# GEGLU gate and value in seven half-size products from block 4 on, with shared staging, in a fused cosformer attention and GEGLU kernel on one core

## The chip, the cores and the metric

One core of a Trainium2 chip. The metric is the device time of one execution in microseconds (us). The kernel before took 314.08 us, the median of three runs (313.26, 314.08, 315.52). The profiled execution has a span of 311.0 us, and all durations below are from it.

TensorE (PE) multiplies matrices into PSUM, which has eight banks of 128 x 512 f32. VectorE (DVE), ScalarE (ACT) and GpSimd (POOL) work on tiles, and SyncE (SP) issues most transfers. Each engine works its own instructions in order, and semaphores make it wait for others.

## What is computed

```python
# q, k, v: (8, 8, 576, 64); phi(x) = [relu(x) cos(theta), relu(x) sin(theta)], theta = pi/2 * s/576
q_p, k_p = phi(q), phi(k)                       # 128 features a head
kv = einsum('bhsf,bhsd->bhfd', k_p, v)
z = sum(k_p, axis=2)
num = einsum('bhsf,bhfd->bhsd', q_p, kv)
den = einsum('bhsf,bhf->bhs', q_p, z) + 1e-6
x = (num / den) -> (4608, 512)                  # 8 batches of 576 rows, 8 heads of 64
out = (gelu(x @ w_gate) * (x @ w_val)) @ w_out  # 512 -> 1536 -> 512
```

Inputs and output are f32; the matmuls take bf16 and sum in f32.

## The kernel before, in words

The 4608 rows of x are cut into nine blocks of 512 (n = 0 to 8). A block's gate and value are made in twelve units of 128 columns of d_ff (jt = 0 to 11, here also called slots, because the other work is placed between units). The order of all work is written out by hand (`tc.manual_schedule`): each engine's instructions run in the order in which the program issues them.

**Standard unit** (`gv_unit`, L392): four matmuls of 128 x 512 for the gate into one bank, four for the value into the next, ACT's gelu (L409), and DVE's product of the two into hT (L410). Units take turns on banks 0, 1 and 2, 3.

**Output product** (`product`, L503). The output of block n - 1 is made during block n, in two halves p of the rows, each in seven half-size products in place of eight (Winograd's form of Strassen's method). A product is six matmuls of 128 x 256 (L510). The slots of one half make products 2 and 1, 5, 6, 7, 4 and 3 in turn. Sums S1 to S4 of parts of hT are made on DVE (`h_sum`, L494), sums of the weights T1 to T4 once. ACT copies products 1, 6 and 7 to SBUF (u, L528), and DVE adds them to others (L524). Rows are stored by SP (L421).

**Attention** of batch b = n + 1 is done in the slots of block n. q and k are scaled by cosine on DVE (L163) and by sine on ACT (L161), 128 x 256 at a time, from f32 staging places (two buffers for each of q, k, v) that SP loads (`loads`, L81) two batches ahead. q is transposed by DMA (`turn_q`, L194); `kv_unit` (L242) makes kv in 72 small matmuls; `nm_unit` makes one of five tiles of num and den (8 matmuls, L283, always in banks 6 and 7 from block 2 on), and DVE makes den, its reciprocal and x (L294 to L296); x is transposed by DMA (`turn_x`, L350). In the blocks from 4 on kv is in slot 1, the nm's in slots 2 to 6, q's transposes in slot 8, and the scalings of batch n + 2 in slots 7 to 11; in block 3 batch 5's q is scaled in slots 5 to 9 and its k in slots 10, 11 and block 4's slot 0, after the load of both in slot 11 of block 2.

**Fast unit** (`fast_unit`, L599). The last 28 units, from slot 8 of block 6 on (`FAST`, L557), make gate and value as one 2 x 2 product: [w_gate; w_val], cut in two along d_model, times the block's rows cut in two. Seven products of two 128 x 256 matmuls each (L611) take the place of eight. This needs sums of the weights (`w_sum`, L575) and of x (`x_sum`, L591), and partial results pass through ACT copies and DVE adds. Unit t's first products are woven with the last ones of unit t - 1. The sums of the weights are made in blocks 5 and 6 and lie in the freed staging places of q, k and v.

Of the kernel before, what the change touches and what calls it, by code (L numbers as in the profile page):

```python
# [16 lines left out]
def kernel(  # L17
# [33 lines left out]
    inp = ctx.enter_context(tc.tile_pool(name="inp", bufs=2))  # L51
# [6 lines left out]
    outp = ctx.enter_context(tc.tile_pool(name="outp", bufs=4))  # L58
    psum = ctx.enter_context(tc.tile_pool(name="psum", bufs=1, space=bass.MemoryType.PSUM))
# [17 lines left out]

    def load(eng, name, b, m0, m1, j0=0, j1=R):
        if (name, b) not in staged:
            staged[name, b] = inp.tile([128, NP, R * D], FP32, name=name + "f")  # L80
        eng.dma_start(  # L81
            out=staged[name, b][:, m0:m1, j0 * D:j1 * D],
            in_=rows(srcs[name], b)[:, m0:m1, j0 * D:j1 * D],
        )
# [3 lines left out]
    wo_sb = weights.tile([128, JT, C], BF16)  # L88
    wg_r = moe_w_gate.rearrange("(ct p) j -> p ct j", p=128)
# [23 lines left out]
    dummy = consts.tile([128, BLK], BF16)  # L113
# [32 lines left out]
    phi = {}  # L146

    def phi_tile(name, b):
        if (name, b) not in phi:
            phi[name, b] = attn.tile([128, NP, R, F], BF16, name=name + "p")  # L150
        return phi[name, b]

    def prep(name, b, part, js, m0=0, m1=NP, eng=None):
# [3 lines left out]
        for j in js:  # L157
            o = dst[:, m0:m1, j, part * D:(part + 1) * D]
            i = src[:, m0:m1, j * D:(j + 1) * D]
            if eng is nc.scalar:  # L160
                nc.scalar.activation(o, i, AF.Relu, scale=tab[:, j:j + 1])  # L161
            else:
                (eng or nc.vector).tensor_scalar(  # L163
                    o, i, 0.0, tab[:, j:j + 1], op0=ALU.max, op1=ALU.mult
                )

# [225 lines left out]
    def gv_unit(n, jt, c0=0, w=BLK):  # L392
        xt = xT[n]
        js = slice(jt * 128, (jt + 1) * 128)
        b0 = 2 * (turn[0] % 2)
        turn[0] += 1
        if n not in hT:
            hT[n] = ffn.tile([128, JT, BLK], BF16, name="hT")
        for g, wt in ((0, wg_sb), (1, wv_sb)):
            for ct in range(CT):  # L400
                nc.tensor.matmul(  # L401
                    bank(b0 + g)[:, 0:w],
# [5 lines left out]
        gel = ffn.tile([128, BLK], FP32, name="gel")  # L408
        nc.scalar.activation(gel[:, 0:w], bank(b0)[:, 0:w], AF.Gelu)  # L409
        nc.vector.tensor_mul(  # L410
            hT[n][:, jt, c0:c0 + w], gel[:, 0:w], bank(b0 + 1)[:, 0:w]
# [58 lines left out]
    hs, rest = {}, {}  # L470

    def place(n, p, name, cols, dtype):

        if n < NB - 1:
            return sums.tile([128, cols], dtype, name=name)
        was = "kp" if name[0] == "u" else ("kf", "vf")[p]
        if was not in rest:
            pool, n_el = (attn, 8 * CH) if was == "kp" else (inp, 4 * JH * 128)
            rest[was] = [pool.tile([128, n_el], dtype, name=was), 0]
        t, at = rest[was]  # L480
        rest[was][1] += cols
        return t[:, at:at + cols]
# [74 lines left out]
    FAST = (NB - 3) * JT + 8  # L557
    UNITS = NB * JT - FAST
    CP = CT // 2
    wa, xb, temps = {}, {}, {}  # L560

    def w_sum(name, j0, j1, eng=nc.vector):
        if not wa:
            wa["A11"], wa["A12"] = wg_sb[:, 0:CP], wg_sb[:, CP:CT]
            wa["A21"], wa["A22"] = wv_sb[:, 0:CP], wv_sb[:, CP:CT]
        if name not in wa:
            was = {"S1": "qf", "S2": "qf", "S3": "kf", "S4": "vf"}[name]
            wa[name] = inp.tile([128, CP, J], BF16, name=was)
# [6 lines left out]
        eng.tensor_tensor(  # L575
            wa[name][:, :, j0:j1], wa[x][:, :, j0:j1], wa[y][:, :, j0:j1], op=op
        )

    def x_sum(n, i):
        if n not in xb:  # L580
            xt = xT[n]
            xb[n] = {
                "B11": xt[:, 0:CP, 0:256], "B12": xt[:, 0:CP, 256:512],
                "B21": xt[:, CP:CT, 0:256], "B22": xt[:, CP:CT, 256:512],
            }
        if "x" not in temps:
            temps["x"] = attn.tile([128, 2, 4, CP, 256], BF16, name="qp")
        b = xb[n]
        x, y = (("B12", "B11"), ("B22", "T1"), ("B22", "B12"), ("B21", "T2"))[i]
        b[f"T{i + 1}"] = temps["x"][:, n % 2, i]  # L590
        nc.vector.tensor_tensor(b[f"T{i + 1}"], b[x], b[y], op=ALU.subtract)  # L591
# [5 lines left out]
    gels = {}  # L597

    def fast_unit(t, between):  # L599


        def at(i, t):
            if i == 2:
                return ps[:, 0, 256 * (t % 2):256 * (t % 2) + 256]
            return bank((3, 1)[t % 2] if i in (3, 5) else (2, 6, 7)[t % 3])[:, 0:256]

        def mm(i, t):
            n, jt = divmod(FAST + t, JT)
            a, b = GV[i]
            for ct in range(CP):  # L610
                nc.tensor.matmul(  # L611
                    at(i, t),
                    lhsT=wa[a][:, ct, jt * 128:(jt + 1) * 128],
                    rhs=xb[n][b][:, ct],
                    start=(ct == 0 and i in (1, 5)),
                    stop=(ct == CP - 1),
                    skip_group_check=i not in (1, 5),
                )

        def tmp(i, t):  # L620
            if "t" not in temps:
                temps["t"] = attn.tile([128, 6, 256], FP32, name="qT")
            return temps["t"][:, 2 * i + t % 2]

        def h(t, half):
            n, jt = divmod(FAST + t, JT)
            if n not in hT:
                hT[n] = ffn.tile([128, JT, BLK], BF16, name="hT")
            return hT[n][:, jt, 256 * half:256 * half + 256]

        def gelu(t, half, src):
            if t not in gels:
                gels[t] = ffn.tile([128, BLK], FP32, name="gel")
            nc.scalar.activation(gels[t][:, 256 * half:256 * half + 256], src, AF.Gelu)

        new, old = t < UNITS, t > 0
        M5, U6, G2 = range(3)
        if new:
            mm(1, t)
            nc.scalar.copy(at(2, t), at(1, t))  # L640
            mm(5, t)
            nc.scalar.copy(tmp(M5, t), at(5, t))
        if old:
            mm(7, t - 1)
            gelu(t - 1, 1, tmp(G2, t - 1))
            nc.vector.tensor_tensor(at(3, t - 1), tmp(M5, t - 1), at(7, t - 1), op=ALU.add)
            nc.vector.tensor_tensor(
                h(t - 1, 1), gels[t - 1][:, 256:512], at(3, t - 1), op=ALU.mult
            )
        between()  # L650
        if new:
            mm(6, t)
            nc.scalar.copy(tmp(U6, t), at(6, t))
            mm(2, t)
            gelu(t, 0, at(2, t))
            mm(3, t)
            nc.vector.tensor_tensor(tmp(G2, t), tmp(U6, t), at(3, t), op=ALU.add)
        if old:
            mm(4, t - 1)
            nc.vector.tensor_tensor(  # L660
                h(t - 1, 0), gels[t - 1][:, 0:256], at(4, t - 1), op=ALU.mult
            )
# [33 lines left out]
    for name in ("q", "k"):  # L696
        for m in (0, 2):
            load(nc.gpsimd, name, 2, m, m + 2)
    for m in (0, 2):
        load(nc.gpsimd, "v", 2, m, m + 2)  # L700
# [54 lines left out]
    for jt in range(2, 4):  # L755
        gv_unit(0, jt)
        prep("q", 0, jt - 2, (R - 1,), eng=nc.scalar)
    q1 = {9: (0, 1, 2), 10: (3, 4, 5), 11: (6, 7, 8)}
    for jt in range(4, JT):
        gv_unit(0, jt)  # L760
        if jt == 5:
# [5 lines left out]
        if jt in q1:  # L767
            prep("q", 1, 0, q1[jt])
            prep("q", 1, 1, q1[jt], eng=nc.scalar)

# [267 lines left out]
```

## Time and profile before

| | before |
|---|---|
| runs | 313.26, 314.08, 315.52 us |
| span of the profiled execution | 311.0 us |
| instructions | 7704 |
| units: standard, fast | 80, 28 |
| mean of a standard unit's gelu on ACT, 128 x 512 | 593 ns |
| mean of a scaling on ACT, 128 x 256 | 498 ns |
| landing time of a k load, of 12 on SP | 7.2 us median on the page |
| landing time of an output store | 2.5 us |

The profile has no figure of the profiled execution's own time apart from its span; the runs lie 2.3 to 4.5 us above it. A line such as `L401 PE MATMUL ps<-xT,wv_sb 128*128 128x512 bf16 (+1 forms) x338 | 80.6, 359 | 0.2` gives the source line, the engine, output and inputs by tile name, the shape, how many there were, busy time in us, mean ns of one, and the engine's idle time before them. The 40 slices of the span show when engines work:

```profile
PE   8889999999999999999999999999999999999993
DVE  5954686699897997799688878899899787978782
ACT  7854685966564763365525932593328787787830
POOL 6775420000000000000000000000007991297310
```

Each digit is the busy share of 7.8 us, in tenths. POOL has nothing to do between the first loads and the sums of the weights.

### The profile page before, as it was taken

The numbers are of one execution on the slowest core, as the hardware profiler recorded it, in microseconds if no ns is written. First come the engines' busy times: TensorE is split into PE (matmuls) and PEld (weight loads), VectorE is DVE, ScalarE is ACT, GpSimd is POOL, SyncE is SP. The second block draws the span as 40 slices with busy tenths as digits, with TensorE's granted clock in tenths as the row PEclk, the third lists the DMA queues.
The fourth block names the chain that finished last, engine by engine and source line by source line (L and its number), as shares of the span: only waits on it lengthen the run. The fifth ranks groups of instructions, "written<-read, shape, count | busy, mean of one in ns | idle before, by whom it ended". The sixth has DMA issues, their size and how long they took to land.

```text
span 311.0 us, 7704 instructions
## 1 busy us (share of the span) xinstructions
PE 301.0 (97%) x2867; PEld 208.2 (67%) x2895; DVE 246.8 (79%) x622; ACT 186.6 (60%) x468; POOL 67.9 (22%) x70
## 2 busy tenths in 40 slices
PE   8889999999999999999999999999999999999993
PEld 3574456645876676666666566656668888888882
DVE  5954686699897997799688878899899787978782
ACT  7854685966564763365525932593328787787830
POOL 6775420000000000000000000000007991297310
PEclk9999999999999999999999999999999999999999
DMA  7999999971798956993898589538442111202034
GB/s 277 247 186 246 313 315 412 273 145 37 217 225 260 315 132 153 368 232 94 259 291 177 116 277 303 112 83 124 93 106 52 40 32 41 50 21 69 3 80 123
DMA packets 69077, 53.65 MB, mean 172 GB/s; under 512 B 45392, under 2 KB 54352, under 8 KB 69040
## 3 DMA queue, kind: packets, MB, share of 16 engines
q1 hardware_dynamic: 59264, 41.17, 52.0%
q0 software_dynamic: 9696, 11.93, 16.5%
q8 instruction: 22, 0.36, 0.5%
q14 instruction: 15, 0.12, 0.1%
q10 hardware_dynamic: 80, 0.07, 0.1%
HBM read 37.75 MB, written 9.44 MB: 152 GB/s over the span
## 4 chain that ended last, share of the span: by engine, by line
PE 87%; DMA 4%; issue 4%; POOL 2%; DVE 0%; SPq 0%; ACT 0%; POOLq 0%; ACTq 0%; DVEq 0%
PE ps L401 43%; PE ps L510 20%; PE ps L611 13%; PE ps L431 3%; PE ps L283 3%; PE ps L242 3%; DMA vf<-in_v_dram 2%; DMA wv_sb<-in_moe_w_val_dram 2%; POOL kf L494 1%; PE ps L373 1%; PE ps L205 1%; PE ps L358 0%; SPq L81 0%; POOL gate L679 0%; POOL wg_sb L95 0%
## 5 line engine op out<-in xcount | busy, mean ns | idle before, releaser
L401 PE MATMUL ps<-xT,wv_sb 128*128 128x512 bf16 (+1 forms) x338 | 80.6, 359 | 0.2
L401 PE MATMUL ps<-xT,wg_sb 128*128 128x512 bf16 (+1 forms) x326 | 79.5, 358 | 1.1 <-issue 0.3
L409 ACT ACTIVATE gel<-ps 128x512 f32<-128x512 f32 (+1 forms) x86 | 47.7, 556 | 46.5 <-PE ps L401 43.3
L410 DVE TENSOR_TENSOR hT<-gel,ps 128x512 bf16<-128x512 f32 (+1 forms) x86 | 54.0, 633 | 24.0 <-PE ps L401 19.2
L401 PEld LDWEIGHTS <-wv_sb 128*128 128x128 bf16 x344 | 33.6, 98 | 33.9
L401 PEld LDWEIGHTS <-wg_sb 128*128 128x128 bf16 x344 | 30.7, 98 | 20.9 <-issue 0.2
L974 POOL CAST gate<-qp 128x1 f32<-128x1 bf16 x1 | 0.2, 175 | 190.7 <-DVE qp L591 190.7
L510 PEld LDWEIGHTS <-S 128*128 128x128 bf16 x336 | 32.9, 98 | 10.9 <-DVE S L494 0.6
L528 ACT COPY u<-ps 128x256 f32<-128x256 f32 x42 | 15.6, 372 | 31.4 <-PE ps L510 30.8
L510 PE MATMUL ps<-T,S 128*128 128x256 bf16 x252 | 34.4, 273 | 0.0
L161 ACT ACTIVATE qp<-qf,sin_t 128x256 bf16<-128x256 f32 x72 | 32.1, 502 | 3.4 <-DMA qf<-in_q_dram 3.4
L510 PEld LDWEIGHTS <-hT 128*128 128x128 bf16 x288 | 28.2, 98 | 6.9
L524 DVE TENSOR_TENSOR o_sb<-u,ps 128x256 f32<-128x256 f32 x56 | 23.3, 416 | 10.5 <-ACT u L528 10.3
L161 ACT ACTIVATE kp<-kf,sin_t 128x256 bf16<-128x256 f32 (+1 forms) x73 | 30.0, 480 | 0.9 <-DMA kf<-in_k_dram 0.9
L296 DVE TENSOR_TENSOR x_sb<-ps,rec 128x512 bf16<-128x512 f32 x38 | 26.3, 691 | 1.8 <-DMA xT<-x_sb 0.6
L510 PE MATMUL ps<-wo_sb,hT 128*128 128x256 bf16 x192 | 23.7, 273 | 0.0
L163 DVE TENSOR_SCALAR qp<-qf,cos_t 128x256 bf16<-128x256 f32 x71 | 21.5, 350 | 2.3 <-DMA qf<-in_q_dram 2.3
L611 PE MATMUL ps<-qp,qf 128*128 128x256 bf16 x112 | 21.4, 273 | 0.1
L611 PE MATMUL ps<-xT,wg_sb 128*128 128x256 bf16 x112 | 21.4, 273 | 0.0
L163 DVE TENSOR_SCALAR kp<-kf,cos_t 128x256 bf16<-128x256 f32 x63 | 18.3, 347 | 0.0
L283 PEld LDWEIGHTS <-qT 128*128 128x128 bf16 x304 | 14.6, 98 | 2.7 <-ACT qT L707 0.3
L283 PE MATMUL ps<-kv_sb,qT 128*128 128x65 bf16 x304 | 16.0, 194 | 0.0
(121 smaller groups left out, 457.6 us busy)
## 6 DMA issues: line engine op xcount, KB each, us to landing
out_dram<-o_sb SPq DMA_DIRECT2D x69, 128.0 KB, 2.5
kf<-in_k_dram SPq DMA_DIRECT2D x12, 576.0 KB, 7.2
vf<-in_v_dram SPq DMA_DIRECT2D x12, 576.0 KB, 9.0
qf<-in_q_dram SPq DMA_DIRECT2D x10, 576.0 KB, 5.2
qf<-in_q_dram POOLq DMA_DIRECT2D x4, 576.0 KB, 12.1
kf<-in_k_dram POOLq DMA_DIRECT2D x4, 576.0 KB, 12.8
vf<-in_v_dram POOLq DMA_DIRECT2D x4, 576.0 KB, 12.9
wg_sb<-in_moe_w_gate_dram POOLq DMA_DIRECT2D x6, 256.0 KB, 6.9
```

Of the source, the lines that this page charges most:

```text
L161: nc.scalar.activation(o, i, AF.Relu, scale=tab[:, j:j + 1])
L163: (eng or nc.vector).tensor_scalar(o, i, 0.0, tab[:, j:j + 1], op0=ALU.max, op1=ALU.mult)
L242: nc.tensor.matmul(bank(6 + i)[:, m * (D + 1):(m + 1) * (D + 1)], lhsT=kp[rr, m, j, :], rhs=vx[rr, m, j, :], start=(j == 0), stop=(j == R ...
L283: nc.tensor.matmul(bank(b0 + h // 4)[:, (h % 4) * (D + 1):(h % 4 + 1) * (D + 1)], lhsT=q_cols(b, t, h), rhs=kv_sb[b][:, h // 2, h % 2, :], ...
L296: nc.vector.tensor_tensor(x, nm[:, :, :, 0:D], rec[:, :, :, None].to_broadcast([128, 2, 4, D]), op=ALU.mult,)
L401: nc.tensor.matmul(bank(b0 + g)[:, 0:w], lhsT=wt[:, ct, js], rhs=xt[:, ct, c0:c0 + w], start=(ct == 0), stop=(ct == CT - 1),)
L409: nc.scalar.activation(gel[:, 0:w], bank(b0)[:, 0:w], AF.Gelu)
L410: nc.vector.tensor_mul(hT[n][:, jt, c0:c0 + w], gel[:, 0:w], bank(b0 + 1)[:, 0:w])
L510: nc.tensor.matmul(at, lhsT=hs.setdefault(key, h_parts(n, p))[a][:, j], rhs=ts[b][:, j], start=(j == 0 and i in (1, 2, 4, 5)), stop=(j == ...
L524: nc.vector.tensor_tensor(o, got[key, k], x, op=op)
L528: nc.scalar.copy(got[key, i], at)
L611: nc.tensor.matmul(at(i, t), lhsT=wa[a][:, ct, jt * 128:(jt + 1) * 128], rhs=xb[n][b][:, ct], start=(ct == 0 and i in (1, 5)), stop=(ct == ...
```

## The change

- From block 4 on, gate and value are made in seven products for 50 units. A `Pair` is two fast units side by side: each of its seven steps is four 128 x 256 matmuls into one full bank (left half one unit, right half the other), and its ACT and DVE instructions are 512 wide. p1 goes to the sum bank and is copied by ACT to bank 1; p5 goes to bank 3 and is copied to SBUF (m5); p6 is summed on the sum bank and DVE adds m5 into bank 3; p2 is summed onto bank 1 and gelu taken; p3 is summed onto bank 3 and gelu taken (gel1); after p7 DVE adds m5 and multiplies with gel1 (h1); after p4 DVE multiplies with the first gelu (h0).
- Blocks 4 and 5 are four `group`s each, block 6 has two: a pair, woven with the work of three slots (x, y, z) and one standard unit in banks 2 and 1, whose value products come after z and p4. The rest of block 6 and blocks 7 and 8 are pairs in `fast_step`, which weaves a pair's steps with those of the pair before, alternately on banks 0 and 2 as the sum bank.
- `prep_both` scales q and k of a batch in one 128 x 512 instruction, for batches 5 to 7, from block 3's slot 4 on; in blocks 4 and 5 by the table `PREPS` (s and c on ACT, C on DVE). In block 3, DVE has all cosines and ACT all sines.
- The staging places of q, k and v become single (`st`); some early batches lie in places that later hold sums (`sm`, `fs`). The loads follow a table, `LOADS`.
- Sums of x and the casts of v from block 4 on move to GpSimd. Of the sums of the weights, columns 0 to 1023 are made on DVE in blocks 0 and 1, the rest on GpSimd in blocks 5 and 6.
- In blocks 4 to 6 the nm's are in slots 3 to 7 (before 2 to 6), and q's transposes in slot 11.

The diff, cut to its core:

```diff
-    inp = ctx.enter_context(tc.tile_pool(name="inp", bufs=2))
+    inp = ctx.enter_context(tc.tile_pool(name="inp", bufs=1))
...
+    st = inp.tile([128, 3, NP, R * D], FP32)
+    sm = sums.tile([128, NP * R * D], FP32)
+    fs = fast.tile([128, 6 * BLK], FP32)
...
+    def prep_both(b, part, j, eng):
...
+        o = phis[:, :, :, j, part * D:(part + 1) * D].rearrange("p a m d -> p (a m) d")
+        i = st[:, 0:2, :, j * D:(j + 1) * D].rearrange("p a m d -> p (a m) d")
+        tab = (cos_t, sin_t)[part]
+        if eng is nc.scalar:
+            nc.scalar.activation(o, i, AF.Relu, scale=tab[:, j:j + 1])
+        else:
+            eng.tensor_scalar(o, i, 0.0, tab[:, j:j + 1], op0=ALU.max, op1=ALU.mult)
...
-    def gv_unit(n, jt, c0=0, w=BLK):
+    def gv_unit(n, jt, c0=0, w=BLK, to=None, between=None):
...
+            if g == 0:
+                gel = ffn.tile([128, BLK], FP32, name="gel")
+                nc.scalar.activation(gel[:, 0:w], bank(to[0])[:, 0:w], AF.Gelu)
+                if between:
+                    between()
...
-    FAST = (NB - 3) * JT + 8
-    UNITS = NB * JT - FAST
...
-    def x_sum(n, i):
+    def x_sum(n, i, eng=nc.gpsimd):
...
+    class Pair:
+        def __init__(self, n, T, sum_bank=0, m5=0):
+            self.n, self.js = n, (2 * T, 2 * T + 1)
+            self.sum = bank(sum_bank)
+            self.m5 = fs[:, (4 + m5) * BLK:(5 + m5) * BLK]
+        def mm(self, i):
+            to = {2: bank(OTHER), 3: bank(MIX), 5: bank(MIX)}.get(i, self.sum)
             a, b = GV[i]
...
+            for half, j in enumerate(self.js):
+                for ct in range(CP):
+                    nc.tensor.matmul(
+                        to[:, 256 * half:256 * half + 256],
+                        lhsT=w_part(a, j * 128, (j + 1) * 128)[:, ct],
+                        rhs=xb[self.n][b][:, ct],
...
+        def p1(self):
+            self.mm(1)
+            nc.scalar.copy(bank(OTHER), self.sum)
+        def p5(self):
+            self.mm(5)
+            nc.scalar.copy(self.m5, bank(MIX))
+        def p6(self):
+            self.mm(6)
+            nc.vector.tensor_tensor(bank(MIX), self.m5, self.sum, op=ALU.add)
+        def p2(self):
+            self.mm(2)
+            self.gel0 = ffn.tile([128, BLK], FP32, name="gel")
+            nc.scalar.activation(self.gel0, bank(OTHER), AF.Gelu)
+        def p3(self):
+            self.mm(3)
+            nc.scalar.activation(gel1, bank(MIX), AF.Gelu)
+        def p7(self, val):
+            self.mm(7)
+            nc.vector.tensor_tensor(bank(val), self.m5, self.sum, op=ALU.add)
+            nc.vector.tensor_tensor(self.h(1), both(gel1), both(bank(val)), op=ALU.mult)
+        def p4(self):
+            self.mm(4)
+            nc.vector.tensor_tensor(self.h(0), both(self.gel0), both(self.sum), op=ALU.mult)
...
+    def group(n, g, x, y, z):
+        f = Pair(n, g)
+        f.p1()
+        f.p5()
+        x()
+        f.p6()
+        f.p2()
+        y()
+        f.p3()
+        f.p7(OTHER)
+        def between():
+            z()
+            f.p4()
+        gv_unit(n, 8 + g, to=(2, OTHER), between=between)
+    def fast_step(new, old, a=None, b=None):
         if new:
+            new.p1()
         if old:
+            old.p7(6)
         if new:
+            new.p5()
+        if a:
+            a()
+        if new:
+            new.p6()
         if old:
+            old.p4()
+        if new:
+            new.p2()
+        if b:
+            b()
+        if new:
+            new.p3()
...
+    early_sums = {5: ("S1", 0), 6: ("S1", 512), 7: ("S3", 0), 8: ("S3", 512)}
     for jt in range(4, JT):
         gv_unit(0, jt)
+        if jt in early_sums:
+            name, j0 = early_sums[jt]
+            w_sum(name, j0, j0 + 512)
...
-        + [("q8", 2), ("o", 1, 4), ("o", 2, 4), ("kv",), ("q2", 0, 2), ("o", 3, 4)]
+        + [("q8", 2), ("o", 1, 4), ("w", "S2", 0), ("o", 2, 4), ("kv",), ("q2", 0, 2)]
+        + [("o", 3, 4), ("w", "S2", 512)]
...
-        + [("q2", 2, 3), ("o", 2, 8), ("xt", 1, 5), ("nm", 3, 6), ("q2", 3, 4), ("o", 3, 8)]
+        + [("q2", 2, 3), ("w", "S4", 0), ("o", 2, 8), ("xt", 1, 5), ("nm", 3, 6), ("q2", 3, 4)]
+        + [("w", "S4", 512), ("o", 3, 8)]
...
-            5: [("q", 5, js(0, 2))], 7: [("q", 5, js(2, 5))], 8: [("q", 5, js(5, 8))],
-            9: [("q", 5, js(8, 9))],
-            10: [("k", 5, js(0, 3)), ("v", 5, 0)], 11: [("k", 5, js(3, 6)), ("v", 5, 2)],
+            4: [("qk", 5, js(0, 1))], 5: [("qk", 5, js(1, 2))], 6: [("qk", 5, js(2, 4))],
+            7: [("qk", 5, js(4, 6))], 8: [("qk", 5, js(6, 8))], 9: [("qk", 5, js(8, 9))],
+            10: [("v", 5, 0)], 11: [("v", 5, 2)],
...
+    LOADS = {
+        (1, 11): [(3, "k"), (3, "v")],
+        (2, 1): [(4, "q")], (2, 6): [(4, "k"), (4, "v")],
+        (2, 11): [(5, "q")], (3, 1): [(5, "k")], (3, 2): [(5, "v")],
+        (3, 9): [(6, "q"), (6, "k")], (4, 0): [(6, "v")],
+        (4, 8): [(7, "q", 0, 4), (7, "k", 0, 4), (7, "v")],
+        (5, 0): [(7, "q", 4, R), (7, "k", 4, R)],
+    }
...
+    PREPS = {
+        3: "s0", 4: "c0 C1", 5: "s1 s2 c2", 6: "s3", 7: "c3 C4", 8: "s4 s5 c5",
+        9: "s6 C6", 10: "s7 C7", 11: "s8 c8",
+    }
+    def attention(n, jt):
...
+        t_nm = 3
+        if 0 <= jt - t_nm - 1 < late_of(b):
+            turn_x(b, jt - t_nm - 1)
+        if 0 <= jt - t_nm < NT:
+            nm_unit(b, jt - t_nm)
+        if jt == 1:
+            kv_unit(b)
...
+            for what in PREPS.get(jt, "").split():
+                eng = nc.vector if what[0] == "C" else nc.scalar
+                prep_both(b + 1, "cs".index(what[0].lower()), int(what[1]), eng)
+            if jt in (6, 7):
+                m = 2 * (jt - 6)
+                cast_v(b + 1, m, m + 2, nc.gpsimd.tensor_copy)
+            if jt == 11:
+                turn_q(b + 1)
+        start_loads(n, jt)
+    def slot(n, jt):
+        o_n, o_jt = (n, jt) if n < 7 else divmod(n * JT + jt - 1, JT)
+        if (n, jt) != (7, 0):
+            o_step(o_n, o_jt)
+        attention(n, jt)
+        more(n, jt)
...
+        groups = {4: 4, 5: 4, 6: 2}.get(n, 0)
+        for g in range(groups):
+            group(n, g, *slots(n, 3 * g, 3 * g + 1, 3 * g + 2))
+        pairs = {4: (), 5: (), 6: (2, 3, 5)}.get(n, range(JT // 2))
+        for i, T in enumerate(pairs):
+            new = Pair(n, T, 2 * (made % 2), made % 2)
+            made += 1
+            at = 3 * groups + 2 * i
+            fast_step(new, old, *slots(n, at, at + 1))
+            old = new
```

## The prediction, as it was put on record

> **What bounds the kernel now.** I read first the page's busy shares and chain, then busy time by block, then chain and timelines inside block 4.
>
> ```profile
> PE 301.0 (97%) x2867; PEld 208.2 (67%) x2895; DVE 246.8 (79%) x622; ACT 186.6 (60%) x468; POOL 67.9 (22%) x70
> PE 87%; DMA 4%; issue 4%; POOL 2%; DVE 0%; SPq 0%; ACT 0%; POOLq 0%; ACTq 0%; DVEq 0%
> ```
>
> TensorE sets the time; Vector is on the chain for 0%. By block (3, 4, 5, 6 as far as it is standard, then the fast part to 297):
>
> ```profile
> core 0: us, PE busy (x) PEld busy (x) DVE busy (x) ACT busy (x) POOL busy (x), PEclk, DMA share, GB/s
> 112.00:144.60 32.60, 32.34 (x304) 21.37 (x307) 27.41 (x70) 16.88 (x40) 0.00 (x0) 1.00 0.78 199
> 144.60:177.20 32.60, 32.28 (x290) 20.01 (x292) 25.85 (x67) 17.93 (x42) 0.00 (x0) 1.00 0.86 207
> 177.20:209.70 32.50, 32.29 (x289) 20.05 (x292) 27.23 (x67) 16.75 (x39) 0.00 (x0) 1.00 0.74 193
> 241.30:297.00 55.70, 55.64 (x511) 49.72 (x509) 44.86 (x119) 42.49 (x133) 34.97 (x23) 1.00 0.15 36
> ```
>
> A block costs 32.55, with TensorE nearly full, while Vector is busy for 26 to 27 of it. The chain has no gap and gives TensorE's prices:
>
> ```profile
> 154.07 1.73 PE ps L401 x8
> 155.80 0.65 PE ps L510 x6
> 156.45 0.26 PE ps L283 x8
> ...
> 244.85 1.53 PE ps L611 x14
> ```
>
> A standard unit takes 1.73, a fast unit 1.53, an output product 0.65, a num/den unit ("nm") 0.26. So the 22 units that become fast save 22 x (1.727 - 1.53) = 4.3.
>
> Vector's prices, from start to start:
>
> ```profile
> 157.23 0.55 DVE L494 TENSOR_TENSOR S<-hT 128x768 bf16<-128x768 bf16 x1
> 157.70 0.16 DVE L294 TENSOR_SCALAR den<-ps 128x8 f32<-128x8 f32 x1
> 157.89 0.20 DVE L295 RECIPROCAL rec<-den 128x8 f32<-128x8 f32 x1
> 158.13 0.69 DVE L296 TENSOR_TENSOR x_sb<-ps,rec 128x512 bf16<-128x512 f32 x1
> 158.74 0.68 DVE L410 TENSOR_TENSOR hT<-gel,ps 128x512 bf16<-128x512 f32 x1
> 159.33 0.41 DVE L524 TENSOR_TENSOR o_sb<-u,ps 128x256 f32<-128x256 f32 x1
> 159.66 0.55 DVE L494 TENSOR_TENSOR S<-S,hT 128x768 bf16<-128x768 bf16 x1
> 148.93 0.87 DVE L163 TENSOR_SCALAR kp<-kf,cos_t 128x256 bf16<-128x256 f32 x3
> ```
>
> S sum 0.47; den, rec and x of an nm 1.04 together; a 512-wide op on PSUM 0.61; output add 0.34; a 256-wide scaling 0.27. A merged 512-wide scaling isn't shown: between 0.27 and 0.54; I take 0.48 (nearest: two at 0.27, less a fixed cost of 0.07, which is what a 512-wide op saves on two 256-wide adds, 2 x 0.34 - 0.61). An add whose result the next instruction reads: 0.72, its own 0.69 and a little.
>
> **The change, part by part. Blocks 4 and 5.** Each is four groups of three slots; a group is seven 4-matmul steps (7 x 0.437 = 3.06), a standard unit (1.73), and the slots' products and nm's. TensorE alone: group 0 8.7 (four products, kv 1.27), group 1 7.5 (three products, three nm's), group 2 7.9 (four, two nm's), group 3 6.75 (three): 30.9, against 32.55. But Vector works in program order, and now the group's own TensorE steps wait for it: p3 for the add behind p6, the standard unit's value products for h1 (same bank), the next group's p1 for h0 (bank 0), each nm for the x before it, since all nm's share banks 6 and 7.
>
> Vector's queue in group 1: output add 0.34, S5 0.47, nm 1.04, p6 add 0.61, output add 0.34, S6 0.47, nm 1.04, scaling 0.48, p7 add 0.72, h1 0.61, output add 0.34, S7 0.47, nm 1.04, h0 0.61 = 8.58. The first add can't start before p1, p5 and product 7 have run (1.53), their result has reached ACT (about 0.25 from a matmul's end to ACT's start, e.g. 293.6 to 293.85), and ACT has copied u (0.37): at 2.2. So h0 ends at 10.8 and p1 of the next group starts at 10.9: 3.4 over TensorE's 7.5. Vector's total is no excess (26.2 a block): it is uneven, and TensorE can't run a group ahead.
>
> Group 0: product 5 needs S1, queued behind the add that waits for u1: ready at 3.7, TensorE there at 3.05; with the h0 gate 9.5 (+0.8). Group 2: an nm stands before the p6 add and the next waits for its x: 9.25 (+1.3). Group 3: 7.6 (+0.8; two scalings before p7's add). Sum 37.3, so +4.7 for each block: +9.4. Bounds for a block: -1.6 (no stall) to +6.4 (each dependent step also pays a second 0.25).
>
> **Block 6**: two groups (9.5 + 10.4; no scalings), three pairs (5.9 + 4.4 + 4.4): 34.9 against 31.6 before, plus 0.4 because a pair, not a unit, is left open at its end: +3.7 (-0.9 to +5). **Blocks 7 and 8**: same TensorE work as before; p5 waits for gelu on its bank, which is ready 0.25 + 0.60 + some ACT delay after p3, while p1 and p7 cover 0.87: about 0.05 in each of 12 steps, +0.6 (0 to 2). **Tail** +0.2 (one pair's last steps instead of one unit's).
>
> **Block 3** keeps standard units, but its scalings of q and k of batch 5 are now merged from slot 4, so they need k at once. SP's queue before:
>
> ```profile
> 114.62 7.50 SPq L194 DMA_TRANSPOSE qT<-qp  x2
> 122.16 1.13 SPq L81 DMA_DIRECT2D qf<-in_q_dram  x2
> 123.33 2.74 SPq L81 DMA_DIRECT2D kf<-in_k_dram  x2
> 126.13 1.10 SPq L81 DMA_DIRECT2D vf<-in_v_dram  x2
> 127.34 3.27 SPq L350 DMA_TRANSPOSE xT<-x_sb  x2
> ```
>
> Behind qT (two transposes, 3.7 each) q is issued until 123.3 as before, but k moves from slot 11 of block 2 to slot 1 of block 3, past two xT transposes (1.6 each) and two stores (0.55 each): issued at 127.2 to 128.4. k's landing takes 3.7 to 13.7, median 7.7 for this tile, but q's and v's transfers no longer run at its side: I take about 4.5, landing at 132.5 (131.5 to 136). Already before, ACT stands idle 2.38 until 129.90 for q. Now Vector and ACT both stand at the slot-4 scaling; behind it queue the unit muls, u copies and nm's. nm in slot 5 still runs at 128.24; its x waits behind the scaling, and the nm of slot 6 (131.54 before) must wait for it: scaling 0.48, mul 0.61, o add, S, nm chain and the second scaling come to 3.3 after landing: 135.8, TensorE idle 4.3, then 0.3 more: +4.6 (2.5 to 8). v and the stores behind k are hidden: v is cast only in slots 10 and 11, after 139.
>
> **Blocks 0 and 1**: four w_sums of 512 columns (two for S1, two for S3) among units 5 to 8 of block 0, four in the transition (S2, S4). The same sums of 128x1024 in blocks 5 and 6 took 0.68 on Vector: 8 x 0.68 = 5.4. TensorE's standard units and ACT's output copies cover most of it; two in the transition stand directly ahead of an nm's chain, and half of each shows: +0.5 (0 to 1.0). The x_sums, v casts and late parts move to GpSimd, empty before from 40 to 205 us (0.00 in the windows), at 1.16 to 2.12 each: 0 for itself (0 to 2). The loads' new places, other than k's, count 0: each has over 1 us to its first use. So do qT's transposes, from slot 8 to slot 11, with the first nm from slot 2 to 3: some 13 us lie between, against 7.5 of issue, 1.7 to landing (5.4 - 3.7) and some 2.3 of xT's and stores on SP. If one is late, 1 to 3, as for k. Merged scalings take 9 x (0.54 - 0.48) off Vector and about 9 x 0.2 off ACT: 0, since ACT isn't the bound. Single-buffered staging acts through the load times, counted above.
>
> Sum: blocks 4 and 5 +9.4, 6 +3.7, 7 and 8 +0.6, block 3 +4.6, 0 and 1 +0.5, tail +0.2 = +19.0 on the profiled span of 311.0. The median of the three runs is 314.08, 3.1 above the span; the same 3.1 is kept: 333. All lower ends together give 314.1 - 1.4 = 312.7, all upper ones +34, 348; I don't take them to fall together.
>
> **Two rules of the Trainium skill.** The trace: from 235 to 244 GpSimd's sums (128x1024, 2.12) leave Vector's adds at 0.41 to 0.43, but at 4.6 GpSimd's 128x128 scalings took 1.42 and 1.85 beside Vector's scalings of SBUF data. "SBUF — State Buffer", "Who interferes with whom", says that GpSimd and Vector lock each other out when Vector works with two SBUF inputs or in its fast modes: S sums, or scalings. It speaks against x_sums on GpSimd: an estimate from the page would add up to 1.2 to a Vector queue per sum, 12 sums. My sum has 0. And the granted clock is 1.00 in all windows above; "TensorE: Matmul & The Clock Gate", Part 1, has an idle of some 3.4 us halve the clock: block 3's stall would reach that, an estimate of 1.7 more (half of one such window). No row here shows it.
>
> **Rivals.**
> - B: k is in time in block 3 (lands by 129.9, as q did), the queues are as above: 333 - 4.6 = 328.5. For it: a load's minimum of 3.7. Against: its place in SP's queue.
> - C, GpSimd's sums hold up Vector: 12 x_sums by 0.43 (1.85 - 1.42) to 1.16 (a whole sum) each, +5 to +14: 338 to 347; at 0.7 each 341. For it: the scalings at 4.6; against: Vector's 0.41 unchanged at 235 to 244.
> - A, other side: the queues don't gate TensorE. It decides at group 1: were Vector's 8.58 behind the first add no more than 5.3 (7.5 - 2.2), TensorE would set the pace: 314.1 - 4.3 + 4.6 = 314.4, or 309.8 with k in time. For it: 26.2 of Vector in 30.9. Against: group 1 holds 9.2 of them with the previous mul.
>
> **How the numbers follow.** Likeliest, queues and k both late, 333 (own range 327 to 339): 0.64. B 0.15. C 0.12. A 0.09, half faster, half within 1%. Three runs of before span 0.7%, so about 1% can be told from no change. The range 321 to 341 leaves out A and half of C. Slower: 0.64 + 0.15 + 0.12 = 0.91, less 0.02 for B's lower end: 0.89; same 0.06, faster 0.05.
>
> **What would show it.** Product 2 of slot 0 in block 5 against block 4: 37.3 apart (30.9 if wrong). In group 1, TensorE idle with Vector as releaser, some 3.4 in all. In block 3, ACT and Vector released by k's load. Vector well over 0% on the chain. Wrong if TensorE stays at 97% busy, or the stalls sit on ACT or on a load that I gave 0.

## The result, and the profile after

The changed kernel takes 341.21 us, the median of four runs (339.26 to 343.41), against 313.67 before (312.63 to 315.52): a ratio of 1.0878, 95% interval 1.0809 to 1.0947. It is slower by 27.5 us. The prediction had 333.0 (+19) and a range to 341.0, so the median stands 0.2 above its upper end. The profiled execution has a span of 338.0, 27.0 over the 311.0 of before, and stands 3.2 below its median (before: 2.7 below the 313.67). Sums by block below are on spans. Four of the kernels below had one execution over 1.5% above the kernel's fastest: the ratios leave it out, the medians don't, and the profiles of the first and of the last experiment are of such an execution.

First the page of the changed kernel, busy time and the shares of the chain:

```profile
PE 304.8 (90%) x3000; PEld 222.1 (66%) x3027; DVE 243.4 (72%) x535; ACT 187.3 (55%) x389; POOL 97.4 (29%) x93
PE 49%; DMA 18%; DVE 14%; issue 7%; SPq 4%; POOL 3%; ACT 3%; POOLq 0%; DVEq 0%; ACTq 0%
```

TensorE's share of the span falls from 97% to 90%, and of the chain from 87% to 49%; transfers and Vector take its place there. Then busy time by block: block 3, 4, 5, and all from block 6 on (start and end, span, then busy time of PE, PEld, DVE, ACT and POOL with the number of instructions, granted clock, DMA share, GB/s).

```profile
113.20:155.10 41.90, 34.69 (x308) 22.17 (x310) 28.96 (x68) 16.75 (x35) 4.77 (x4) 0.92 0.57 153
155.10:193.30 38.20, 32.79 (x338) 24.78 (x341) 27.61 (x57) 22.27 (x42) 8.83 (x8) 1.00 0.88 240
193.30:231.40 38.10, 32.72 (x338) 24.78 (x341) 26.98 (x55) 22.54 (x43) 13.95 (x9) 1.00 0.44 109
231.40:338.00 106.60, 96.57 (x939) 82.92 (x939) 69.64 (x132) 49.98 (x98) 42.18 (x30) 0.99 0.27 60
```

Vector is busy for 27.6 and 27.0 of blocks 4 and 5, against 25.9 and 27.2 before, hardly more, yet TensorE stands idle for 5.4 in each. From the first matmul of a block to that of the next, the four stretches of before are 32.7, 32.6, 32.6 and 101.4 and now 41.9, 38.2, 38.0 and 106.6, so the 27.0 are: 1.4 before block 3, 9.2 in block 3, 5.7 in block 4, 5.5 in block 5, 5.2 after. What TensorE waited for between 113 and 232 (total, times, longest; the five largest):

```profile
PE ps L312 <- DVE x_sb L325: 10.2, 5, 6.7
PE ps L649 <- DVE hT L694: 2.8, 2, 1.4
PE ps L649 <- DVE ps L676: 1.8, 6, 0.5
PE ps L546 <- DVE sm L530: 1.0, 2, 0.5
PE ps L431 <- DVE hT L690: 0.9, 3, 0.5
```

These are the waits that the prediction named: an nm for the x before it, p1 for h0, p3 for p6's add, product 5 for S1, the value products for h1. In the same blocks of before (112 to 210) the list has one line:

```profile
PE ps L401 <- issue: 0.2, 1, 0.2
```

The 6.7 is in block 3. SP's queue there, then Vector, then TensorE:

```profile
115.93 7.53 SPq L223 DMA_TRANSPOSE qT<-phis  x2
123.50 2.49 SPq L97 DMA_DIRECT2D st<-in_q_dram  x2
126.11 2.54 SPq L379 DMA_TRANSPOSE xT<-x_sb  x2
128.71 1.22 SPq L454 DMA_DIRECT2D out_dram<-o_sb  x2
130.04 1.06 SPq L97 DMA_DIRECT2D st<-in_k_dram  x2
131.20 1.03 SPq L97 DMA_DIRECT2D st<-in_v_dram  x2
```

```profile
136.76 0.49 DVE L194 TENSOR_SCALAR phis<-st,cos_t 128x512 bf16<-128x512 f32 x1 [8.11 <-DMA st<-in_k_dram]
```

```profile
131.91 1.47 PE L546 MATMUL ps<-wo_sb,hT 128*128 128x256 bf16 x12
140.09 0.60 PE L312 MATMUL ps<-kv_sb,qT 128*128 128x65 bf16 x8 [6.70 <-DVE x_sb L325]
140.50 1.90 PE L431 MATMUL ps<-xT,wg_sb 128*128 128x512 bf16 x4
142.19 1.91 PE L431 MATMUL ps<-xT,wv_sb 128*128 128x512 bf16 x4
143.90 1.08 PE L546 MATMUL ps<-T,sm 128*128 128x256 bf16 x6
144.81 0.42 PE L312 MATMUL ps<-kv_sb,qT 128*128 128x65 bf16 x8
145.07 1.02 PE L431 MATMUL ps<-xT,wg_sb 128*128 128x512 bf16 x3
```

k stands behind all of these but v in SP's queue, lands at 136.7, and holds Vector for 8.11 at the merged scaling. TensorE then waits 6.70, and after that its 512-wide matmuls take twice as long: four need 1.90 where four need 1.03 otherwise, and the product 1.08 for 0.82. The granted clock is 0.54 from 140.09 to 144.81 (0.92 over the whole block); that work takes 4.72 where before it took 2.64, so the slow phase costs 2.1. With the 6.70 these are most of the 9.2.

### The profile page after: what moved, and what is told of

The parts are those of the page before. It is cut to its first block, busy times and chain, and to the rows that moved or that the text cites. A ratio compares the mean times of both kernels' runs of the same rounds, so it can differ in the third digit from the quotient of the medians.

```text
span 338.0 us, 7782 instructions
## 1 busy us (share of the span) xinstructions
PE 304.8 (90%) x3000; PEld 222.1 (66%) x3027; DVE 243.4 (72%) x535; ACT 187.3 (55%) x389; POOL 97.4 (29%) x93
## 4 chain that ended last, share of the span: by engine, by line
PE 49%; DMA 18%; DVE 14%; issue 7%; SPq 4%; POOL 3%; ACT 3%; POOLq 0%; DVEq 0%; ACTq 0%
PE ps L431 18%; PE ps L649 15%; PE ps L546 12%; DMA st<-in_q_dram 5%; DMA st<-in_k_dram 4%; DMA wo_sb<-in_moe_w_out_dram 4%; SPq L223 3%; DMA st<-in_v_dram 2%; DVE sm L530 2%; DVE o_sb L560 2%; DMA wv_sb<-in_moe_w_val_dram 2%; DVE x_sb L325 2%; DVE ps L676 2%; PE ps L271 1%; DVE hT L690 1%
## 5 line engine op out<-in xcount | busy, mean ns | idle before, releaser
L431 PE MATMUL ps<-xT,wv_sb 128*128 128x512 bf16 (+1 forms) x253 | 59.4, 356 | 1.2 <-DVE hT L690 0.9
L431 PE MATMUL ps<-xT,wg_sb 128*128 128x512 bf16 (+1 forms) x236 | 56.6, 354 | 1.3 <-DMA xT<-x_sb 0.2
L560 DVE TENSOR_TENSOR o_sb<-sm,ps 128x256 f32<-128x256 f32 x56 | 23.4, 418 | 27.9 <-ACT sm L564 27.8
L546 PEld LDWEIGHTS <-sm 128*128 128x128 bf16 x336 | 32.8, 98 | 11.3 <-DVE sm L530 2.4
L546 PE MATMUL ps<-T,sm 128*128 128x256 bf16 x252 | 34.7, 274 | 1.5 <-DVE sm L530 1.5
L649 PEld LDWEIGHTS <-ws 128*128 128x128 bf16 x320 | 30.4, 98 | 7.2 <-issue 3.3
L649 PE MATMUL ps<-fs,ws 128*128 128x256 bf16 x240 | 34.7, 273 | 0.0
L179 ACT ACTIVATE phis<-st,sin_t 128x256 bf16<-128x256 f32 (+1 forms) x75 | 31.5, 484 | 1.8 <-DMA st<-in_q_dram 1.1
L689 DVE TENSOR_TENSOR ps<-fs,ps 128x512 f32<-128x512 f32 x25 | 17.4, 694 | 18.9 <-PE ps L649 18.0
L192 ACT ACTIVATE phis<-st,sin_t 128x512 bf16<-128x512 f32 x27 | 18.8, 723 | 13.4 <-DMA st<-in_k_dram 13.4
```

What stands on the lines that cost most here:

```text
L431: nc.tensor.matmul(bank(to[g])[:, 0:w], lhsT=wt[:, ct, js], rhs=xt[:, ct, c0:c0 + w], start=(ct == 0), stop=(ct == CT - 1),)
L546: nc.tensor.matmul(at, lhsT=hs.setdefault(key, h_parts(n, p))[a][:, j], rhs=ts[b][:, j], start=(j == 0 and i in (1, 2, 4, 5)), stop=(j == ...
L560: nc.vector.tensor_tensor(o, got[key, k], x, op=op)
L649: nc.tensor.matmul(to[:, 256 * half:256 * half + 256], lhsT=w_part(a, j * 128, (j + 1) * 128)[:, ct], rhs=xb[self.n][b][:, ct], start=(hal ...
L689: nc.vector.tensor_tensor(bank(val), self.m5, self.sum, op=ALU.add)
```

## The experiments

All kernels are the changed one with the edit shown, timed against the kernel before (ratios are to it).

**k of batch 5 from another queue.**

```diff
-                    load(nc.sync, name, b, m, m + 2)
+                    load(nc.gpsimd if (b, name) == (5, "k") else nc.sync, name, b, m, m + 2)
```

> The changed kernel with one edit: k of batch 5 is loaded by GpSimd's queue, which is empty then, in place of SP's; same point of the program. Theory (block 3 is long because k's load stands behind qT's transposes, q's load, two xT transposes and stores on SP and lands at 136.6): k lands before 130, the nm of slot 6 no longer stands idle for 6.7, and the clock doesn't fall; about 8 to 9 less, 333 against 341.2. Rival (q's load, also behind qT, lands as late as k, or the merged scalings themselves are too much for Vector there): less than 4 goes, 337 or more.

Measured: 342.34, ratio 1.0868 (1.0779 to 1.0957), no gain. Its runs spread from 338 to 348. In the profiled execution (span 345.5) k was issued at 119.2, but its second half landed 17.4 after its issue, and SP's queue was slower:

```profile
114.83 10.13 SPq L223 DMA_TRANSPOSE qT<-phis  x2
125.01 1.42 SPq L97 DMA_DIRECT2D st<-in_q_dram  x2
126.54 9.09 SPq L379 DMA_TRANSPOSE xT<-x_sb  x2
```

qT's transposes took 10.13 for 7.53 and xT's 9.09 for 2.54; TensorE waited 7.60 for qT and Vector until 141.1 for q. The theory in its simple form (only k's place on SP) fails by the time. That a load and transposes in flight together hold each other up is a reading of this one execution; the next experiment bears on it.

**k right behind q on SP.** Batch 4's last k scalings move one slot ahead, so that k's single place is free.

```diff
-            10: [("k", 4, js(0, 3))], 11: [("k", 4, js(3, 6))],
+            10: [("k", 4, js(0, 3))], 11: [("k", 4, js(3, 9))],
...
-        (2, 11): [(5, "q")], (3, 1): [(5, "k")], (3, 2): [(5, "v")],
+        (2, 11): [(5, "q"), (5, "k")], (3, 2): [(5, "v")],
```

> The changed kernel with batch 4's last k scalings in slot 11 of block 2 in place of block 3's slot 0, which frees k's place, and batch 5's k loaded by SP right behind q, ahead of two xT transposes and two stores. Theory (it is the place in SP's queue that makes k late): k is issued by 126.5 and lands near 132, the wait before the nm of slot 6 falls from 6.7 to 2 to 3 and the clock falls less or not: 335 to 337. Rival (transfers share what is there: k beside q makes q, or the xT transposes behind it, late): k or q lands after 135, 340 or more.

Measured: 338.51 (1.0778, 1.0730 to 1.0826), 2.7 less, half of what was expected. k was issued by 126.8 and landed at 134.4, 7.6 later; the wait fell to 4.38, and the clock fell all the same (0.52 from 137.75 to 142.67). So some 2.3 of the stall is k's place in the queue. Ahead of the two xT transposes k's two loads landed 7.5 and 7.8 after their issue (5.2 and 6.0 in the changed kernel, behind them), and the two transposes 7.5 (median) in place of 5.0: here load and transposes did hold each other up.

**Block 3's scalings apart.**

```diff
-            4: [("qk", 5, js(0, 1))], 5: [("qk", 5, js(1, 2))], 6: [("qk", 5, js(2, 4))],
-            7: [("qk", 5, js(4, 6))], 8: [("qk", 5, js(6, 8))], 9: [("qk", 5, js(8, 9))],
+            5: [("q", 5, js(0, 2))], 7: [("q", 5, js(2, 5))],
+            8: [("q", 5, js(5, 8)), ("k", 5, js(0, 4))], 9: [("q", 5, js(8, 9)), ("k", 5, js(4, 9))],
```

> The changed kernel with block 3's scalings of batch 5 apart again: q in slots 5, 7, 8, 9 as before the change, k in slots 8 and 9, 256 wide each; k's load stays late on SP. Theory (it is the merged scaling at slot 4 that pulls k's due time ahead of its landing): the idle before the nm of slot 6 goes, some 0 to 1 is left at slot 8, 333 to 334. Rival (a late transfer on SP holds something else in block 3, such as x or stores): the stall stays, 338 or more.

Measured: 336.81 (1.0732, 1.0705 to 1.0759), 4.4 less. The 6.70 is gone with k issued no earlier (131.39), which shows that the merged scaling pulled k's due time ahead. But a new wait of 3.57 came at block 4's start. Vector there, and GpSimd:

```profile
144.44 5.31 DVE L181 TENSOR_SCALAR phis<-st,cos_t 128x256 bf16<-128x256 f32 x6
149.68 0.67 DVE L443 TENSOR_TENSOR hT<-gel,ps 128x512 bf16<-128x512 f32 x1
```

```profile
144.79 1.28 POOL L629 TENSOR_TENSOR fs<-xT 128x512 bf16<-128x512 bf16 x1 [99.16 <-DVE phis L181]
146.14 1.15 POOL L629 TENSOR_TENSOR fs<-xT,fs 128x512 bf16<-128x512 bf16 x1
147.25 1.20 POOL L629 TENSOR_TENSOR fs<-xT 128x512 bf16<-128x512 bf16 x1
148.41 1.19 POOL L629 TENSOR_TENSOR fs<-xT,fs 128x512 bf16<-128x512 bf16 x1
```

Six scalings of 0.27 each took 5.31, and ended when GpSimd's four sums did. What else could hold them, such as k's landing, the next experiment tests.

**The same, and block 4's sums of x on Vector.**

```diff
-                x_sum(*what)
+                x_sum(*what, eng=nc.vector if what[0] == 4 else nc.gpsimd)
```

> As the run with block 3's scalings apart, and block 4's four sums of x on Vector in place of GpSimd. There six scalings took 5.31 while GpSimd made these sums, and block 4's first step waited 3.57 for Vector. Theory (GpSimd and Vector keep each other from SBUF): the six take 1.7, the four sums 0.42 each; the wait falls below 1.8, 334.5 to 335.5 against 336.8. Rival (the scalings were slow or late for another reason, such as k's landing): they stay over 4 and the time at 337 or, with 1.7 more on Vector, 338.

Measured: 334.48 (1.0647, 1.0592 to 1.0702), as the theory had it: six scalings took 1.66, the sums 0.42 each, and two waits of 1.00 and 0.80 are left. GpSimd's hold is shown.

```profile
144.86 1.66 DVE L181 TENSOR_SCALAR phis<-st,cos_t 128x256 bf16<-128x256 f32 x6
```

**GpSimd's work as fills.** Sums of x, casts of v and late sums of weights become fills, which read nothing and are shorter (0.52 for 1.15, 1.03 for 1.15, 0.95 for 2.12); the results of that work are left out.

```diff
-        eng.tensor_tensor(b[f"T{i + 1}"], b[x], b[y], op=ALU.subtract)
+        if n == 8:
+            eng.tensor_tensor(b[f"T{i + 1}"], b[x], b[y], op=ALU.subtract)
+        else:
+            eng.memset(b[f"T{i + 1}"], 0.0)
...
-                w_sum(*what, eng=nc.gpsimd)
+                nc.gpsimd.memset(w_part(*what), 0.0)
...
-                cast_v(b + 1, m, m + 2, nc.gpsimd.tensor_copy)
+                cast_v(b + 1, m, m + 2, lambda o, i: nc.gpsimd.memset(o, 0.0))
```

> The changed kernel with the sums of x, the casts of v and the late sums of the weights on GpSimd in blocks 3 to 7 replaced by fills with zeros of the same places, which read nothing (their results are left out). Theory (GpSimd's reading holds up Vector's scalings and sums by some 3 in all in this kernel, and about half of it is on the path): Vector's 128x512 scalings all take 0.5, and 1 to 2 go, 339.5. Rival (the hold on SBUF is a main cause of the long blocks): 336 or less; or none: 341 with scalings as long as before.

Measured: 337.24 (1.0749, 1.0698 to 1.0800), 4.0 less, between theory and rival; the span is 2.2 less. All 17 scalings of 128x512 took 0.476 to 0.486 (up to 1.37 in the changed kernel), and blocks 4 and 5 are 37.3 each in place of 38.2 and 38.0. Whether it is the reading or the length of GpSimd's work that counts, this run doesn't tell: the fills are short, and some start at other times.

**Standard units in blocks 4 and 5.**

```diff
-        groups = {4: 4, 5: 4, 6: 2}.get(n, 0)
+        groups = {6: 2}.get(n, 0)
+        if n < 6:
+            for jt in range(JT):
+                gv_unit(n, jt)
+                slot(n, jt)
+            continue
```

> The changed kernel with standard units in blocks 4 and 5 in place of the groups, all other work in the same slots (the sums of x for these blocks are still made and not used). Theory (the groups make Vector's queue gate TensorE, 38.2 and 38.0 a block against 32.55): each block falls to 32.6 to 33.5, about 9 to 11 less, 330 to 332. Rival (single staging and the loads' new times, or GpSimd's work, make these blocks long): they stay over 36, and the total is 337 or more.

Measured: 332.38 (1.0589, 1.0561 to 1.0617), 8.8 less. Block 5 is back at 32.6; block 4 stays at 36.7, because ACT waits 3.35 for batch 6's k in the merged scaling of its slot 3, and TensorE 2.29 behind it. So block 5's groups cost 5.4, near the 4.7 that was said, and in block 4 they had covered a late load: there ACT waited 3.46 for the same k in the changed kernel too.

**S5 to S8 on GpSimd.**

```diff
-            eng = nc.gpsimd if n > 6 else nc.vector
+            eng = nc.gpsimd if n > 6 or n > 3 and jt in (3, 4, 5, 6) else nc.vector
```

> The changed kernel with the output sums S5 to S8 of blocks 4 to 6 (slots 3 to 6) on GpSimd in place of Vector. Theory (group 1 is as long as Vector's queue): three sums of 0.47 leave it, so group 1 falls from 11.3 to about 9.9 and group 2 from 9.7 to 9.3, 1.9 for each of three blocks, about 5 less: 336. Rival (GpSimd and Vector hold each other up on SBUF, sums of 1.64 beside scalings and sums): less than 2 goes, 339 to 342, and Vector's 128x512 scalings show over 0.6 each.

Measured: 336.43 (1.0736, 1.0672 to 1.0799), 4.8 less; the span 3.8. Block 5's groups 1 and 2 took 9.59 and 9.54 in place of 10.99 and 9.84. The three sums of 0.47 that left group 1's queue shorten it by just their 1.4: Vector's queue sets its time there. In block 4, group 1 gained only 0.2 (11.08 for 11.29): behind ACT, which waits for batch 6's k until 170.29, TensorE waits 0.75 for p7's add. Of the rival there is a part: block 5's group 2 gained 0.3 for 0.47.

**Four repairs together.** To the unmerged scalings, the x sums and S5 to S8 as above come S1 ahead of the output adds and the nm's spread:

```diff
+    NMS = {4: 0, 5: 1, 7: 2, 8: 3, 10: 4}
+    TURNS = {5: 0, 6: 1, 8: 2, 9: 3, 11: 4}
...
+        first = 3 < n < 7 and jt == 0
+        if first:
+            h_sum(n - 1, 0, "S1")
```

> The previous kernel with what is long in the groups taken apart: S5 to S8 of blocks 4 to 6 on GpSimd, S1 ahead of the output adds on Vector, and the five nm's in slots 4, 5, 7, 8 and 10 (in 5 and 8 ahead of the output product) in place of 3 to 7. Theory (Vector's order in group 1 and S1 in group 0 gate TensorE): group 1 falls from 11.3 to about 8.2, group 0 from 9.55 to about 8.9, blocks 4 and 5 to 32.5 to 33.5 each, block 6 by some 2; 320 to 323 in all. Rival (once Vector's queue is shorter, the next thing, GpSimd's hold on SBUF or the loads of batches 6 and 7 into single places, holds the blocks at 36 or more): 328 or more.

Measured: 327.36 (1.0423, 1.0386 to 1.0460), 13.8 less than the changed kernel, but not the 18 to 21 expected. In block 5 (35.1) groups 0 and 1 are 8.85 and 8.58, near what was said, but groups 2 and 3 took 9.4 and 8.2. Two nm's stand in Vector's queue there now, and two scalings beside GpSimd's work took 1.13 and 1.02 in place of 0.48, as the rival had it. Block 4 waits 1.83 once more behind batch 6's k.

**Three parts undone.** Unmerged, block 4's x sums on Vector, and standard units in blocks 4 and 5:

> The changed kernel with three of its parts undone at once: standard units in blocks 4 and 5, block 3's scalings apart, and block 4's sums of x (not used) on Vector. Theory (the costs found apart add up): from 341.2, 8.8 for the groups and 6.7 for block 3 go, 325 to 326; block 4 is still 3 or 4 long because batch 6's k lands late in its single place. Rival (one long block hides another's late loads): more is left, 329 or more.

Measured: 326.05 (1.0402, 1.0345 to 1.0459). The parts add up; ACT's wait for batch 6's k is still there (2.3 of TensorE). Against before, its trace has 2.3 more ahead of block 3, 1.1 in block 3, 3.3 in block 4, none in block 5 and 5.8 from block 6 on.

**Matmuls in the idle time.**

```diff
+            if (n, jt) == (3, 6):
+                for _ in range(40):
+                    nc.tensor.matmul(
+                        ps[:, 5, CH:C], lhsT=ident, rhs=wo_sb[:, 0, 0:CH], start=True, stop=True
+                    )
```

> The changed kernel with 40 matmuls of 128x256 on data at hand (4.4 us, into an unused half bank, results not used) between the products and the nm of block 3's slot 6, where TensorE stands idle for 6.7. Theory (the idle lowers the granted clock: eight matmuls after it took 3.41 in place of 1.73): TensorE idle falls to some 2.3, the clock stays at 1.00 there, the nm starts when it did, and 2.0 go: 339. Rival (the slower matmuls have another cause, or the added ones delay the nm): the same 341, or more.

Measured: 344.23 (1.0959, 1.0887 to 1.1030), no gain. The added matmuls had to wait themselves, for an output add of the same bank, so they stood behind 4.79 of idle and delayed the nm:

```profile
138.23 6.69 PE L1018 MATMUL ps<-wo_sb,ident 128*128 128x256 bf16 x40 [4.79 <-DVE o_sb L560]
144.76 0.42 PE L312 MATMUL ps<-kv_sb,qT 128*128 128x65 bf16 x8
145.02 1.02 PE L431 MATMUL ps<-xT,wg_sb 128*128 128x512 bf16 x4
```

As a way to save the clock it failed. It does show that the slow phase belongs to the time after an idle, not to an instruction: now the added matmuls are the slow ones (6.69 for 40 x 0.109 = 4.4), and the units after them run at full speed.

**The early sums of the weights**, three trials. On GpSimd in block 2 (`w_sum(name, j0, j0 + 512, eng=nc.gpsimd)` in its slots):

> The changed kernel with the eight early sums of the weights on GpSimd in block 2 in place of Vector in blocks 0 and 1. Theory (they cost 0.7 to 1.7 among Vector's other work there): block 2's first product comes at 80.2 to 80.5 in place of 81.7, about 1.2 less, 340. Rivals: nothing goes there (the later start is the first loads' doing), 341; or GpSimd holds up Vector in block 2, and its length grows over 33.3.

Measured: 358.29 (1.1428, 1.1343 to 1.1514), 17 slower. GpSimd had nothing ahead of them and ran all eight at once, from 44.95 to 61.6. Vector then:

```profile
45.55 17.31 DVE L209 CAST vx<-fs 128x1152 bf16<-128x1152 f32 x2
62.78 0.60 DVE L181 TENSOR_SCALAR phis<-st,cos_t 128x256 bf16<-128x256 f32 x2
```

Two casts of 0.75 took 17.31 and TensorE waited 15.35 for v. In place of the question it answers another, below. Left out, their place filled with zeros by GpSimd:

> The changed kernel without the eight early sums of the weights; their place is filled with zeros by GpSimd instead, so gate and value of blocks 4 to 8 are not the reference's. Theory (the sums cost 0.7 to 1.7 in blocks 0 and 1): block 2's first product comes at 80.2 to 80.5 in place of 81.7, 340. Rival (the later start is not theirs but that of the first loads): 81 or later, 341.

Measured: 347.31 (1.1038, 1.0976 to 1.1101), because the fills (7.05) held two scalings of Vector for 8.12; nothing can be said of the start from it. On Vector, one in each of slots 0 to 7 of block 2:

> The changed kernel with the eight early sums of the weights on Vector still, but one in each of slots 0 to 7 of block 2, in place of block 0 and the transition to block 1. Theory (they cost 0.9 to 1.4 where they are, among Vector's work that TensorE waits for): block 2's first product comes at 80.2 to 80.6 in place of 81.7; block 2 has 4.4 of Vector free and grows by less than 0.5; about 1 less, 340. Rival (the late start is the first loads'): 81 or later there.

Measured: 342.02 (1.0916, 1.0841 to 1.0991), no gain. Block 2's first product came at 80.8 in place of 81.7 (before: 80.2). But in the eleven traces here of kernels that have the sums in blocks 0 and 1 it comes anywhere from 80.9 to 82.4, so what the sums cost there is not shown. Block 2 is 35.5 long in place of 33.3 (33.3 to 33.9 in those eleven): about 2 of their 5.4 show, though the block had 4.4 of Vector free.

**Five parts undone.** The early sums moved as in the last trial, and in block 6 `std = {4: 12, 5: 12, 6: 8}.get(n, 0)` standard units:

> As the run with three parts undone, and two more: the early sums of the weights as in the run beside this one, and standard units in slots 0 to 7 of block 6 (pairs from slot 8 on, about where fast units began before the change). What is left of the change is single staging, the loads' table, sums of x and casts on GpSimd and pairs in place of fast units. Theory (the parts add up): 326.0 less 1 for the early sums and 3 to 4 for block 6: 321 to 322.5; the rest over 314 is block 4's late k (3), block 3 (1.5) and block ends. Rival (something not named here still costs): 324 or more.

Measured: 323.59, ratio 1.0300 (1.0242 to 1.0358). The three runs behind the ratio are 321.3 to 324.8, in the mean 322.8, 3.2 below the kernel with three parts undone, with the 2 of block 2 in it that the expectation lacked. With that 2 the parts add up to within about 1. No version here beats the kernel before, and what makes up the last 9 over it is argued in the expectation, not shown: the profile (span 328.0) isn't read by block.

## Why the prediction was right and wrong

| term | predicted | measured |
|---|---|---|
| blocks 0 to 2 | +0.5 | +1.4 |
| block 3 | +4.6 | +9.2 |
| block 4 | +4.7 | +5.7 |
| block 5 | +4.7 | +5.5 |
| block 6 to the end | +4.5 | +5.2 |

Of the 8.0 by which the sum fell short, block 3 gives 4.6.

- **The queues of blocks 4 to 6: right.** The groups of block 4 took 9.55, 11.29, 9.72 and 7.68, against 9.5, 10.9, 9.25 and 7.6. With fills on GpSimd they took 9.54, 11.0, 9.14 and 7.59, in sum 37.27 for the 37.3 of the prediction. Block 6's two groups and three pairs took 9.54, 10.60, 5.80, 4.36 and 4.37, against 9.5, 10.4, 5.9, 4.4 and 4.4. A pair's step takes 0.44 from start to start, so the saving of 0.2 a unit is there too, and pays for little. Group 1 as the trace shows it on TensorE; its waits add up to 2.95, for "some 3.4":

```profile
166.19 0.42 PE L312 MATMUL ps<-kv_sb,qT 128*128 128x65 bf16 x8
...
168.99 0.42 PE L312 MATMUL ps<-kv_sb,qT 128*128 128x65 bf16 x8 [0.86 <-DVE x_sb L325]
169.60 0.60 PE L649 MATMUL ps<-xT,ws 128*128 128x256 bf16 x4 [0.19 <-DVE ps L676]
...
173.52 1.02 PE L431 MATMUL ps<-xT,wv_sb 128*128 128x512 bf16 x4 [0.49 <-DVE hT L690]
175.95 0.60 PE L649 MATMUL ps<-xT,wg_sb 128*128 128x256 bf16 x4 [1.41 <-DVE hT L694]
```

- **Block 3: the step that failed, by the size of k's landing.** The mechanism was the one named: ACT and Vector stood at the merged scaling until k landed, and the nm started 3.4 after that, where 3.3 was reckoned. The prediction had k issued at 127.2 to 128.4 and landed at 132.5, "about 4.5" later, because "q's and v's transfers no longer run at its side". That reason was wrong: v's loads were issued at 131.20, 1.2 behind k's. k was issued from 130.04 and landed at 136.7, 6.7 later. Counted from the start of the block, which begins 1.4 later than before, that is a landing at 135.3, 2.8 late: 0.8 for the issue (q's issue took 2.49 for 1.13) and 2.0 for the landing. The wait was 6.7 for 4.3.
- **The clock: cited, and left out of the sum.** The sum had 0 for the slow phase and a separate estimate of 1.7 by the Trainium skill, "TensorE: Matmul & The Clock Gate", Part 1. Measured are 2.1, nearly half of what block 3 took beyond its 4.6. The rule was the better of the two: "No row here shows it" was no reason against it, because TensorE's longest idle in the blocks shown was 0.2.
- **GpSimd's hold: sized at nothing, at 5 to 14 in the rival C; it is 0.6 to 0.7 for a block.** The runs show it as "SBUF — State Buffer", "Who interferes with whom", of the Trainium skill says: Vector's scalings and casts stand while GpSimd works on SBUF, and its adds with one PSUM operand don't (0.68 beside GpSimd's sums at 213 to 215, as elsewhere). Scalings of 0.48 rose to as much as 1.37 in the changed kernel, and an S sum of 0.55 to 1.03. With the fills, group 2 of blocks 4 and 5 falls from 9.72 and 9.84 to 9.14 and 9.13, and the span by 2.2 in all, part of it elsewhere. Rival C was named for the right cause and priced too high: Vector's busy time is only 1.8 above that with the fills. That C at 0.7 a sum gives the measured 341 is an accident.
- **The other loads: sized at nothing.** Batch 6's k was late in block 4. There that cost some 0.3 (group 1 took 11.29, in block 5 10.99), because the groups were long for another reason; with standard units it is 2.3 of wait and a slow phase.
- **The start: under-sized.** It came 1.4 late for 0.5, and no run shows why.
- **Rivals A and B** did not occur. Vector was busy for 27 of a 38-us block: its average never told that it was the bound.

## What to carry to other kernels

Cost a woven schedule by walking through the in-order queues step by step with the durations and start latencies of the trace; here that gave the four groups of block 4 to within 0.5 us, and to about 0.1 with fills on GpSimd, where the busy share (72%) said that there was room. When two loads' users are merged into one instruction, the later of the two sets the time of all that is queued behind it, on every engine that carries a merged half. Moving work to an idle engine is free only if the two don't hold each other up, as GpSimd and Vector did here.

## What the runs showed of the hardware

- Back-to-back GpSimd instructions kept Vector's f32-to-bf16 cast waiting through all eight of them, 16.6 us, not only through one; four fills in a row (7.05), which read nothing, did the same to two scalings (8.12).
- After an idle of TensorE of 6.70 (the changed kernel), 4.79 (with added matmuls), 4.38 (k behind q) and 3.57 (scalings apart) its matmuls took about twice as long for 3 to 5 us. An idle of 2.29 was followed by such a phase in one kernel (standard units in blocks 4 and 5), which began 1.1 us after work had, and one of 1.83 with 0.49 close behind in another (four repairs); one of 2.32 was followed by none (three parts undone).
- With k's two loads of 576 KB issued ahead of them, two xT transposes landed 7.5 (median) after their issue in place of 5.0, and the loads 7.5 and 7.8 in place of 5.2 and 6.0.
